# Threshold attention and a quick-GELU block on one core: masking moved to ScalarE, sums of weights folded on VectorE, values of a pair in one group

## Chip, core and metric

The kernel runs on one core of a Trainium2 chip. The metric is the device time of one execution in microseconds. Before the change it is 1937.87 us, the median of three runs (1936.68 to 1942.23).

## The reference

Attention over 8 batches and 8 heads with 576 positions of 64 elements, all fp32. A score counts only if it is within tau (0.02) of the largest of its row. Then a block with a quick GELU over the 4608 tokens, whose two weight matrices (512 x 2048 and 2048 x 512) come in as 64-bit floats.

```
scores = scale * q @ k.T
thresh = max(scores, -1) - tau
scores = where(scores >= thresh, scores, -1e9)
attn   = exp(scores - max(scores, -1))
x      = (attn / (sum(attn, -1) + 1e-9)) @ v      # heads side by side: 4608 x 512
h      = x @ w_in
out    = (h / (1 + exp(-1.702 * h))) @ w_out
```

## The kernel before

Two heads of a batch make a pair; there are 32 pairs. Scores are held transposed, with keys on partitions: four main tiles of 128 keys (128 x 1152, two heads side by side) and a tail tile, in which both heads have 64 partitions (128 x 576). Per pair:

- `prep` (L191) transposes q and k on VectorE in 32 x 32 blocks, and copies k's last 64 keys into a block-diagonal tile `kd`.
- `scores` (L207) has TensorE write two PSUM pairs and ScalarE copy them to SBUF. `part_max` (L233) takes maxima over 32 keys. `max_a`, `max_b` and `max_c` (L247 to L283) finish them over two TensorE transposes, and `mb` holds each query's maximum spread over 128 partitions.
- `sub` (L285) subtracts it, `exps` (L297) takes the exponential into another tile, `threshold` (L303) sets to zero what is under the threshold: one VectorE operation over two inputs.
- `values` (L311) multiplies by v on TensorE, tile by tile. `add_w` (L326) adds the tiles on GpSimd, `den_a` (L341) sums over partitions by a matmul with ones. `place_x` (L358) takes the reciprocal of 128 x 576 numbers and writes the scaled values as columns of x.

The second block runs over nine blocks of 512 tokens. A unit of `mm1` is two matmuls of 128x512 with w_in; every second one ends with a tanh on ScalarE (L389) and, on VectorE, gT (L390). A unit of `mm2` is two matmuls with w_out. Each fp32 matmul shows as two records in the trace. The PSUM tiles of both kinds (`hps`, `ops`) share two buffers.

The weights are made fp32 on the chip, in 64 pieces of 128 x 256. `convert_w` (L139) takes 24 bits of the mantissa on VectorE in two operations from both 32-bit words, the exponent in one more, which GpSimd limits and shifts; `convert_w_end` (L173) adds the sign, and GpSimd multiplies.

The order is written by hand, and each engine works through its own queue in that order. A step has a place in a period of 18 for its pair, and the steps are sorted by place (L445 to L497). The scores of one pair lie beside the values of the pair before. Pairs of the first batch have no units beside them; from then on each batch has the units of one block of the batch before. Two blocks are left for the end. All DMAs are issued by SP.

Of the kernel before, what the change touches and what calls it, by code (L numbers as in the profile page):

```python
# [11 lines left out]
U32 = mybir.dt.uint32  # L12
AF = mybir.ActivationFunctionType
# [7 lines left out]
BIG = 3.0e38  # L21


@with_exitstack
def kernel(
# [9 lines left out]
):  # L35

# [34 lines left out]
    psA = ctx.enter_context(tc.tile_pool(name="psA", bufs=2, space=bass.MemoryType.PSUM))  # L71
    psV = ctx.enter_context(tc.tile_pool(name="psV", bufs=1, space=bass.MemoryType.PSUM))
# [7 lines left out]
    ident = const.tile([P, P], FP32, name="ident")  # L80
    ones = const.tile([P, D], FP32, name="ones")
    tau_b = const.tile([P, 1], FP32, name="tau_b")
    neg = const.tile([P, 1], FP32, name="neg")
    scl = const.tile([P, 1], FP32, name="scl")
    ntau = const.tile([P, 1], FP32, name="ntau")
# [4 lines left out]
    def load_pair(n):  # L90
        b, hp = divmod(n, NPAIR)
        raws[n] = []
        for name, src in (("q", q), ("k", k)):
            t = work.tile([P, QB, 32], FP32, name=f"{name}_raw", tag=f"{name}_raw", bufs=1)
            for h in range(2):
                for j in range(2):
                    nc.sync.dma_start(
# [27 lines left out]
    def load_w():  # L125
# [6 lines left out]
        if not wide:  # L132
            nc.sync.dma_start(out=part, in_=dram)
            return
        t = work.tile([P, WC, 2], U32, name="w64", tag="w64", bufs=3)
        nc.sync.dma_start(out=t.rearrange("p c w -> p (c w)"), in_=dram.bitcast(U32))
        staged.append((t, part))

    def convert_w():  # L139

        if not staged:
            return
        t, part = staged.pop(0)
        lo, hi = t[:, :, 0], t[:, :, 1]

        frac = work.tile([P, WC], U32, name="frac", tag="frac")
        nc.vector.tensor_scalar(  # L147
            out=frac, in0=hi, scalar1=0xFFFFF, scalar2=4,
            op0=ALU.bitwise_and, op1=ALU.logical_shift_left,
        )  # L150
        nc.vector.scalar_tensor_tensor(  # L151
            out=frac, in0=lo, scalar=28, in1=frac,
            op0=ALU.logical_shift_right, op1=ALU.bitwise_or,
        )
        mant = work.tile([P, WC], FP32, name="mant", tag="mant")
        nc.scalar.activation(
            out=mant, in_=frac, func=AF.Copy, bias=1.0, scale=2.0**-24
# [31 lines left out]
    mats, sT, stats = {}, {}, {}  # L189

    def prep(n, which):  # L191
# [5 lines left out]
        if which == 1:  # L197
            for h in range(2):
                nc.gpsimd.tensor_copy(  # L199
                    out=kd[n % 2][ts(h, D), ts(h, D)], in_=dst[ts(h, D), MAIN:S]  # L200
                )
            del raws[n]
# [4 lines left out]
    def scores(n, t):  # L207
# [11 lines left out]
        else:  # L219
            st = work.tile([P, 2, S], FP32, name="s_m", tag="s_m", bufs=6)  # L220
# [12 lines left out]
    def part_max(n, t):  # L233

        if t == 0:
            stats[n] = [
                work.tile([P, NKT, 2 * QB], FP32, name="pmax", tag="pmax"),
# [73 lines left out]
    def values(n, t):  # L311
        if t == 0:
            pvs[n] = psV.tile([P, 2, 512], FP32, name="pv", tag="pv")
# [214 lines left out]
```

## Time and profile before

| | |
|---|---|
| median of three runs | 1937.87 us |
| profiled execution | 1936.7 us, of which the span 1934.9 us |
| TensorE, matmuls (PE) | 1596.7 us busy, 83% |
| VectorE (DVE) | 1271.3 us, 66% |
| ScalarE (ACT) | 500.4 us, 26% |
| GpSimd (POOL) | 553.2 us, 29% |
| chain that ended last | PE 50%, DVE 44% of the span |
| DMA | 12.3% of 16 engines' span, 55.47 MB |

The shares are means over stages with different limits, so the stages have to be read one by one. The profiled execution is 1.2 us under the median of the runs.

### The profile page before, as it was taken

Reading aid. Unit: us, or ns where it says so; the run is one execution under the profiler, and the core shown is the slowest. Engines: PE = TensorE matmul, PEld = TensorE weight load, DVE = VectorE, ACT = ScalarE, POOL = GpSimd, SP = SyncE. Lnnn points to the kernel's source line nnn. Section 1 sums busy time; section 2 is a strip of 40 time slices with the busy share of each in tenths; the row PEclk is TensorE's granted clock in tenths of the full one; section 3 lists DMA queues with packets and bytes.
Section 4 is the critical chain, followed back from the end, with each engine's and each line's share of the span. In section 5 each row is a group of like instructions: output and inputs, shape, how many; then the busy total and the mean of one; then the engine's idle time right before and its main releaser. Section 6 shows DMA issues by size and latency. Waiting matters only on the chain.

```text
span 1934.9 us, 14193 instructions
## 1 busy us (share of the span) xinstructions
PE 1596.7 (83%) x5056; PEld 688.1 (36%) x5056; DVE 1271.3 (66%) x1300; ACT 500.4 (26%) x725; POOL 553.2 (29%) x427
## 2 busy tenths in 40 slices
PE   4344477779888998899889998898889988999999
PEld 2122233334333333333333333333333333444444
DVE  7999989886766667766776666667666677521010
ACT  3222223222322223222322223223222332211010
POOL 3555555342222222222222221222222222200000
PEclk9766688889999998899999988999999988999999
DMA  3212222211111111111111110011111110000000
GB/s 81 54 47 57 62 57 62 57 38 30 24 19 23 31 24 19 19 30 30 19 19 28 31 19 5 20 30 24 19 19 29 30 19 6 12 11 6 16 0 22
DMA packets 205079, 55.47 MB, mean 29 GB/s; under 512 B 192208, under 2 KB 192208, under 8 KB 205008
## 3 DMA queue, kind: packets, MB, share of 16 engines
q1 hardware_dynamic: 205008, 54.56, 12.3%
q8 instruction: 40, 0.66, 0.1%
q14 instruction: 31, 0.25, 0.0%
HBM read 45.09 MB, written 9.44 MB: 28 GB/s over the span
## 4 chain that ended last, share of the span: by engine, by line
PE 50%; DVE 44%; issue 2%; ACT 2%; POOL 0%; SPq 0%; DVEq 0%; DMA 0%; ACTq 0%; POOLq 0%
PE ops L398 18%; PE hps L382 16%; DVE s_m L305 9%; DVE s_m L288 8%; PE pv L321 7%; PE ps L224 6%; DVE rc L361 6%; DVE s_t L291 5%; DVE frac L151 3%; DVE ex L177 2%; DVE qkT L195 2%; DVE mb L279 2%; DVE gT L390 2%; PE ps L213 2%; DVE frac L147 2%
## 5 line engine op out<-in xcount | busy, mean ns | idle before, releaser
L382 PE MATMUL hps<-xT,w_in 128*128 128x512 f32 x1152 | 583.8, 652 | 95.1 <-DVE gT L390 95.1
L398 PE MATMUL ops<-w_out,gT 128*128 128x512 f32 x1152 | 541.3, 617 | 27.9 <-DVE gT L390 27.9
L224 PE MATMUL ps<-qkT 64*128 64x288 f32 x1024 | 211.1, 496 | 196.6 <-ACT s_m L230 105.2
L382 PEld LDWEIGHTS hps<-xT,w_in 128*128 128x128 f32 x1152 | 224.6, 205 | 386.8 <-issue 257.6
L390 DVE SCALAR_TENSOR_TENSOR gT<-th,hps 128x512 f32<-128x512 f32 x144 | 98.6, 685 | 342.2 <-ACT th L389 342.2
L398 PEld LDWEIGHTS ops<-w_out,gT 128*128 128x128 f32 x1152 | 215.4, 195 | 295.4 <-issue 260.6
L199 POOL COPY kd<-qkT 64x64 f32<-64x64 f32 x64 | 62.8, 982 | 843.0 <-DVE qkT L195 743.8
L245 DVE TRANSPOSE_TENSOR_REDUCE pmax<-s_m 128x36 f32<-128x1152 f32 x128 | 172.8, 1364 | 117.6 <-ACT s_m L230 117.6
L300 ACT ACTIVATE e<-s_m,scl 128x1152 f32<-128x1152 f32 x128 | 160.7, 1256 | 331.4 <-DVE s_m L288 331.4
L305 DVE SCALAR_TENSOR_TENSOR s_m<-s_m,ntau,e 128x1152 f32<-128x1152 f32 x128 | 237.6, 1856 | 1.0
L224 PEld LDWEIGHTS ps<-qkT 64*128 64x128 f32 x1024 | 118.2, 213 | 306.2 <-issue 146.3
L230 ACT COPY s_m<-ps 128x576 f32<-128x576 f32 x256 | 151.8, 640 | 260.7 <-PE ps L224 260.7
L333 POOL TENSOR_TENSOR ws<-ws,s_m 128x1152 f32<-128x1152 f32 x64 | 183.6, 2868 | 64.6 <-DVE s_m L305 63.1
L288 DVE TENSOR_TENSOR s_m<-s_m,mb 128x1152 f32<-128x1152 f32 x128 | 172.4, 1348 | 2.5
L321 PE MATMUL pv<-s_m,v_m 128*64 128x288 f32 x1024 | 173.4, 465 | 0.0
L389 ACT ACTIVATE th<-hps 128x512 f32<-128x512 f32 x144 | 83.8, 590 | 203.8 <-PE hps L382 203.8
L361 DVE RECIPROCAL rc<-rc 128x576 f32<-128x576 f32 x32 | 119.8, 3745 | 12.5 <-ACT rc L352 12.5
L321 PEld LDWEIGHTS pv<-s_m,v_m 128*64 128x64 f32 x1024 | 69.2, 152 | 133.2 <-issue 109.2
L291 DVE TENSOR_TENSOR s_t<-s_t,mb 64x576 f32<-64x576 f32 x64 | 107.1, 1673 | 0.4
L331 POOL TENSOR_TENSOR ws<-s_m 128x1152 f32<-128x1152 f32 x32 | 90.6, 2830 | 37.9 <-DVE s_m L305 36.0
L337 POOL TENSOR_TENSOR ws<-ws,s_t 64x576 f32<-64x576 f32 x64 | 89.9, 1405 | 13.4 <-DVE s_t L305 9.4
L404 ACT ACTIVATE osb<-ops 128x512 f32<-128x512 f32 x36 | 21.2, 590 | 206.8 <-PE ops L398 206.8
(46 smaller groups left out, 837.3 us busy)
## 6 DMA issues: line engine op xcount, KB each, us to landing
q_raw<-in_q_dram SPq DMA_DIRECT2D x128, 72.0 KB, 2.4
k_raw<-in_k_dram SPq DMA_DIRECT2D x128, 72.0 KB, 2.4
out_dram<-osb SPq DMA_DIRECT2D x36, 256.0 KB, 2.0
v_m<-in_v_dram SPq DMA_DIRECT2D x64, 128.0 KB, 2.4
w<-in_moe_w_in_dram SPq DMA_DIRECT2D x32, 256.0 KB, 2.7
w<-in_moe_w_out_dram SPq DMA_DIRECT2D x32, 256.0 KB, 2.7
v_t<-in_v_dram SPq DMA_DIRECT2D x64, 16.0 KB, 2.1
tau_b<-in_tau_dram SPq DMA_DIRECT2D x1, 0.5 KB, 2.5
```

What stands on the lines that cost most here:

```text
L224: nc.tensor.matmul(ps[h][:, c, 0:SH], lhsT=kT[ts(h, D), ts(t, P)], rhs=qT[ts(h, D), ts(c, SH)], start=True, stop=True,)
L230: nc.scalar.copy(out=halves(st[:, h, :]), in_=ps[h][:, :, 0:SH])
L245: nc.vector.tensor_reduce(out=o, in_=i, axis=AXL.X, op=ALU.max, apply_transpose=True)
L288: nc.vector.tensor_tensor(out=s, in0=s, in1=mb, op=ALU.subtract)
L291: nc.vector.tensor_tensor(out=s[ts(h, D)], in0=s[ts(h, D)], in1=mb[ts(h, D), h, :], op=ALU.subtract)
L300: nc.scalar.activation(out=e, in_=s, func=AF.Exp, scale=scl)
L305: nc.vector.scalar_tensor_tensor(out=s, in0=s, scalar=ntau, in1=es.pop((n, t)), op0=ALU.is_ge, op1=ALU.mult)
L321: nc.tensor.matmul(pvs[n][ts(h, D), c, 0:SH], lhsT=lhsT, rhs=rhs, start=(t == 0), stop=(t == NKT),)
L333: nc.gpsimd.tensor_tensor(out=sums[n], in0=sums[n], in1=w[t], op=ALU.add)
L361: nc.vector.reciprocal(out=rc, in_=rc)
L382: nc.tensor.matmul(hidden[0], lhsT=w_in[:, c, ts(j, P)], rhs=xTs[blk][:, c, :], start=(c == 0), stop=(c == NDC - 1),)
L398: nc.tensor.matmul(acc[0], lhsT=gT[j][:, ts(i, P)], rhs=w_out[:, j, :], start=(j == 0), stop=(j == NFC - 1),)
```

## The change

- **Maxima and thresholds.** The two TensorE transposes go. `over_groups` folds the four groups of 32 partitions on VectorE by short copies and operations on 36 columns; `thresholds` subtracts the gap and spreads the result. `sub` then subtracts the threshold.
- **Masking.** ScalarE's parametric Relu with a slope of 1e30 keeps what is positive and drives what is negative far down; the Exp behind it, in place, has a bias that brings the gap back. The VectorE operation and the second tile `e` go.
- **Sums of weights.** GpSimd's additions go. For pairs 0 to 5 TensorE sums by a second group of 20 matmuls with ones; for the rest VectorE reduces each tile over 32 keys and folds as for the maxima. The reciprocal is taken of 18 columns, then spread.
- **Values.** All 20 matmuls of a pair follow each other, behind the first scores of the next pair. Their PSUM tile comes from the same pool as the scores', which now has three pairs of banks.
- **Weights.** A second load of each piece, shifted by three bytes, brings the mantissa's bits into one word, so one VectorE operation with one input replaces two. Nine conversions stand before the first units, the other 55 in 2.2 periods behind them; in the kernel before they stand in the first seven.
- **Other.** `kd` is copied by ScalarE, the first loads of k are issued by ScalarE's queue, score tiles have seven buffers instead of six. Places run on over all pairs instead of anew per pair.

```diff
-    psA = ctx.enter_context(tc.tile_pool(name="psA", bufs=2, space=bass.MemoryType.PSUM))
-    psV = ctx.enter_context(tc.tile_pool(name="psV", bufs=1, space=bass.MemoryType.PSUM))
+    psA = ctx.enter_context(tc.tile_pool(name="psA", bufs=3, space=bass.MemoryType.PSUM))
...
+        t3 = work.tile([P, WC, 2], U32, name="w64s", tag="w64s", bufs=3)
+        nc.sync.dma_start(
+            out=t3.rearrange("p c w -> p (c w)").bitcast(U8)[:, 0 : 8 * WC - 3],
+            in_=dram.bitcast(U8)[:, 3 : 8 * WC],
+        )
...
+        nc.vector.tensor_single_scalar(
+            out=frac, in_=t3[:, :, 0], scalar=0x0FFFFFFF, op=ALU.bitwise_and
+        )
...
+    def over_groups(n, op):
...
+        for w in (64, 32):
+            nc.vector.tensor_copy(out=o[0:w], in_=r[w : 2 * w])
+            nc.vector.tensor_tensor(out=r[0:w], in0=r[0:w], in1=o[0:w], op=op)
+        return r
...
-        e = work.tile(list(s.shape), FP32, name="e", tag="e")
-        nc.scalar.activation(out=e, in_=s, func=AF.Exp, scale=scl)
...
-        nc.vector.scalar_tensor_tensor(
-            out=s, in0=s, scalar=ntau, in1=es.pop((n, t)), op0=ALU.is_ge, op1=ALU.mult
-        )
...
+        nc.scalar.activation(out=s, in_=s, func=AF.Prelu, alpha=STEEP)
+        nc.scalar.activation(out=s, in_=s, func=AF.Exp, scale=scl, bias=shift)
...
+    def spread(n, r):
+
+        nc.vector.reciprocal(out=r, in_=r)
+        rc = work.tile([P, S], FP32, name="rc", tag="rc")
+        nc.vector.transpose(out=rc, in_=r.unsqueeze(2).to_broadcast([P, QB, 32]))
+        rcs[n] = rc
...
+    for n in range(NP):
+        t0 = LEN * n
+        for t in range(NKT + 1):
+            at(t0 + 1.5 * t, scores, n, t)
+            at(t0 + 1.5 * t + 1.0, in_groups, n, t, ALU.max)
+            at(t0 + 8.7 + 1.3 * t, sub, n, t)
+            at(t0 + 9.0 + 1.3 * t, exps, n, t)
+            if n >= BY_PE:
+                at(t0 + 12.4 + 1.3 * t, in_groups, n, t, ALU.add)
+        at(t0 + 8.0, thresholds, n)
+        at(t0 + 18.6, values, n)
+        at(t0 + 18.7, sums_by_pe if n < BY_PE else sums_by_dve, n)
+        at(t0 + 20.3, place_x, n)
...
+    for blk in range(NBLK):
+        first = ready(blk)
+        last = ready(blk + 1) if blk + 1 < NBLK else first + NPAIR * LEN
...
+            at(first + max(last - first, 1.0) * (u + 0.5) / len(todo), *unit)
...
+                at(begin + 0.7 * LEN * i / (early + 1), convert)
...
+                at(ready(0) + 2.2 * LEN * (i - early) / (len(pieces) - early), convert)
```

How the queues stand is shown at three places. First ScalarE, from the sums' eviction to the last exponential of a pair beside mm1 units; `th` is a unit's tanh, `rc` the sums. Before:

```order
L352 ACTIVATE rc<-den 128x576
L300 ACTIVATE e<-s_m,scl 128x1152
L389 ACTIVATE th<-hps 128x512
L300 ACTIVATE e<-s_m,scl 128x1152 x2
L389 ACTIVATE th<-hps 128x512
L300 ACTIVATE e<-s_m,scl 128x1152
L300 ACTIVATE e<-s_t,scl 128x576
```

With the change, in such a stretch from the second tile on (L300 is now the Prelu, L301 the Exp):

```order
L300 ACTIVATE s_m<-s_m 128x1152
L301 ACTIVATE s_m<-s_m,shift,scl 128x1152
L386 ACTIVATE th<-hps 128x512
L300 ACTIVATE s_m<-s_m 128x1152
L301 ACTIVATE s_m<-s_m,shift,scl 128x1152
L210 COPY kd_88<-qkT 64x64 x2
L300 ACTIVATE s_m<-s_m 128x1152
L301 ACTIVATE s_m<-s_m,shift,scl 128x1152
L386 ACTIVATE th<-hps 128x512
L300 ACTIVATE s_t<-s_t 128x576
L301 ACTIVATE s_t<-s_t,shift,scl 128x576
```

Each exponential has become two instructions, the tanh stands between two tiles as before, and the copies of `kd` are new in this queue.

Then TensorE behind the maxima of a pair beside mm1 units, where the next pair's scores and this pair's values begin. Before:

```order
L275 MATMUL p_3315<-ident,mq 128x36
L382 MATMUL hps<-xT,w_in 128x512 x16
L224 MATMUL ps<-qkT 128x288 x4
L382 MATMUL hps<-xT,w_in 128x512 x2
L321 MATMUL pv<-s_m,v_m 64x288 x4
L224 MATMUL ps<-qkT 128x288 x4
L382 MATMUL hps<-xT,w_in 128x512 x2
L321 MATMUL pv<-s_m,v_m 64x288 x4
```

With the change, from pair 6 on:

```order
L379 MATMUL hps<-xT,w_in 128x512 x22
L233 MATMUL ps<-qkT 128x288 x4
L315 MATMUL pv<-s_m,v_m 64x288 x16
L315 MATMUL pv<-s_t,v_t_89 64x288 x4
L379 MATMUL hps<-xT,w_in 128x512 x2
L233 MATMUL ps<-qkT 128x288 x4
```

Eleven units stand in one piece instead of eight, and the values have moved from between the tiles of scores into one group.

Last VectorE behind a pair's maxima while weights are converted; `mb` is the spread maximum or threshold, `frac` and `ex` belong to the conversion. Before:

```order
L279 STREAM_TRANSPOSE mb<-p_1184 128x1152
L177 SCALAR_TENSOR_TENSOR ex<-w_1064,ex 128x256
L147 TENSOR_SCALAR frac<-w_1101 128x256
L151 SCALAR_TENSOR_TENSOR frac<-w_1101,frac 128x256
L161 TENSOR_SCALAR ex<-w_1101 128x256
L288 TENSOR_TENSOR s_m<-s_m,mb 128x1152
L361 RECIPROCAL rc<-rc 128x576
```

With the change:

```order
L282 STREAM_TRANSPOSE mb<-thr 128x1152
L188 SCALAR_TENSOR_TENSOR ex<-w_990,ex 128x256
L162 TENSOR_SCALAR frac<-w64s 128x256
L172 TENSOR_SCALAR ex<-w_1005 128x256
L387 SCALAR_TENSOR_TENSOR gT_73<-th,hps 128x512
L291 TENSOR_TENSOR s_m<-s_m,mb 128x1152
L188 SCALAR_TENSOR_TENSOR ex<-w_1005,ex 128x256
L162 TENSOR_SCALAR frac<-w64s 128x256
L172 TENSOR_SCALAR ex<-w_1029 128x256
L188 SCALAR_TENSOR_TENSOR ex<-w_1029,ex 128x256
```

A conversion has one operation less, two of them now follow a subtraction, and the reciprocal of 576 columns is no longer in the queue.

## Rows read from the trace of the kernel before

**Rows 1.** Windows by stage: stretch, length, busy per engine (instructions), clock, DMA share, GB/s
```profile
24.00:224.60 200.60, 90.12 (x336) 44.14 (x336) 191.06 (x230) 57.84 (x89) 113.13 (x118) 0.69 0.23 57
224.60:417.50 192.90, 133.87 (x411) 57.07 (x411) 170.01 (x230) 55.28 (x93) 99.66 (x119) 0.82 0.21 55
417.50:1655.60 1238.10, 1084.13 (x3594) 458.96 (x3592) 848.18 (x769) 346.60 (x480) 323.83 (x169) 0.94 0.11 22
1655.60:1720.00 64.40, 64.40 (x192) 27.30 (x192) 30.62 (x28) 10.57 (x13) 12.45 (x5) 1.00 0.04 17
1720.00:1935.00 215.00, 211.13 (x492) 93.11 (x491) 20.61 (x30) 22.69 (x38) 0.00 (x0) 1.00 0.03 10
```
The busy times are, in order, those of PE, PEld (weight loads), DVE, ACT and POOL.

**Rows 2.** The same view: a window with mm1 units, one mostly with mm2
```profile
1134.80:1190.00 55.20, 46.52 (x151) 19.22 (x150) 38.82 (x38) 16.02 (x23) 12.50 (x7) 0.91 0.09 16
...
1242.60:1290.70 48.10, 43.99 (x151) 19.05 (x150) 31.77 (x29) 12.87 (x17) 14.46 (x7) 0.96 0.13 30
```

**Rows 3.** Waits: who for whom, us in total, times, longest
```profile
PE ps L224 <- ACT s_m L230: 105.2, 34, 7.4
...
PE hps L382 <- DVE gT L390: 95.1, 34, 5.3
```

**Rows 4.** Timeline of TensorE from 1126: start, length, instruction, [idle before <-releaser]
```profile
1126.85 1.98 PE L382 MATMUL hps<-xT,w_in 128*128 128x512 f32 x4
1128.77 1.19 PE L321 MATMUL pv<-s_m,v_m 128*64 128x288 f32 x8
...
1138.94 7.13 PE L382 MATMUL hps<-xT,w_in 128*128 128x512 f32 x16
1148.39 2.56 PE L382 MATMUL hps<-xT,w_in 128*128 128x512 f32 x4 [2.32 <-DVE gT L390]
```

**Rows 5.** VectorE's groups by form: busy us, mean ns of one | idle before
```profile
L305 DVE SCALAR_TENSOR_TENSOR s_m<-s_m,ntau,e 128x1152 f32<-128x1152 f32 x128 | 237.6, 1856 | 1.0
...
L245 DVE TRANSPOSE_TENSOR_REDUCE pmax<-s_m 128x36 f32<-128x1152 f32 x128 | 172.8, 1364 | 117.6 <-ACT s_m L230 117.6
L288 DVE TENSOR_TENSOR s_m<-s_m,mb 128x1152 f32<-128x1152 f32 x128 | 172.4, 1348 | 2.5
...
L361 DVE RECIPROCAL rc<-rc 128x576 f32<-128x576 f32 x32 | 119.8, 3745 | 12.5 <-ACT rc L352 12.5
...
L291 DVE TENSOR_TENSOR s_t<-s_t,mb 64x576 f32<-64x576 f32 x64 | 107.1, 1673 | 0.4
L390 DVE SCALAR_TENSOR_TENSOR gT<-th,hps 128x512 f32<-128x512 f32 x144 | 98.6, 685 | 342.2 <-ACT th L389 342.2
...
L279 DVE STREAM_TRANSPOSE mb<-p 128x1152 f32<-128x1152 f32 x32 | 44.3, 1383 | 35.4 <-PE p L275 35.4
...
L250 DVE TENSOR_REDUCE mx<-pmax 128x36 f32<-128x144 f32 x32 | 11.5, 358 | 0.0
L255 DVE TENSOR_TENSOR mx<-mx,pmax_t 64x18 f32<-64x18 f32 x64 | 11.0, 172 | 1.5
```

**Rows 6.** The same view: GpSimd's additions and ScalarE's Exp
```profile
L333 POOL TENSOR_TENSOR ws<-ws,s_m 128x1152 f32<-128x1152 f32 x64 | 183.6, 2868 | 64.6 <-DVE s_m L305 63.1
...
L300 ACT ACTIVATE e<-s_m,scl 128x1152 f32<-128x1152 f32 x128 | 160.7, 1256 | 331.4 <-DVE s_m L288 331.4
```

**Rows 7.** Line L291: ns min/median/max, first and last start us, form
```profile
L291 DVE TENSOR_TENSOR s_t<-s_t,mb x64: 740/791/3086, 41.7 to 1680.4; 64x576 f32<-64x576 f32 x64
```

**Rows 8.** Conversion: two groups by form, then line L177 as in rows 7
```profile
L151 DVE SCALAR_TENSOR_TENSOR frac<-w,frac 128x256 uint32<-128x256 uint32 x64 | 62.4, 974 | 2.2
...
L161 DVE TENSOR_SCALAR ex<-w 128x256 uint32<-128x256 uint32 x64 | 21.7, 338 | 0.0
...
L177 DVE SCALAR_TENSOR_TENSOR ex<-w,ex x64: 375/418/2835, 19.0 to 416.5; 128x256 uint32<-128x256 uint32 x64
```

**Rows 9.** DMA issues: KB each, median us from issue to landing
```profile
w<-in_moe_w_in_dram SPq DMA_DIRECT2D x32, 256.0 KB, 2.7
```

## What I expected before the run

> **What bounds the kernel now.** I first cut the span into stages by the starts of one instruction per pair, the maxima's reduce at L250. One period between two such starts I call a window; there are 32 pairs. Read in each row what is nearly full. From 24.0 to 224.6 us (four windows without matmuls of the second block, 50.2 us each) VectorE is busy 191.1 of 200.6 us: VectorE bounds. From 224.6 to 417.5 (three windows) it is still at 170.0 of 192.9, TensorE at 133.9. From 417.5 to 1655.6 (24 windows of 51.6 us) TensorE is busy 1084 of 1238 us at a granted clock of 0.94, VectorE 848. From 1720 on TensorE alone works, 211 of 215 us at clock 1.00 [rows 1]. In that last stretch nothing can be gained but by fewer matmuls, and the change takes none of those out.
>
> The 24 windows are the largest stage. Two of each four carry mm1 units (w_in, then tanh and gT), two carry mm2 units: the first row shown has mm1 (55.2 us), the second mostly mm2 (48.1 us). Read there that TensorE is busy 46.5 and 44.0 us, VectorE 38.8 and 31.8 [rows 2]. So TensorE is near its limit, and what can be won is its idle time and its half-speed stretches. Who makes it idle stands in the list of waits: ScalarE's evictions of the scores 105.2 us, VectorE's gT 95.1 us [rows 3]. The timeline shows one such wait: a stop of 2.32 us for gT, and the next four matmul records then last 2.56 us instead of 1.98, at the lower granted clock [rows 4].
>
> **The change on each engine.** All durations are of the profiled execution, 1936.7 us with a span of 1934.9; its time is 1.2 us under the median of the three runs, so the sum below stands for the median as well.
>
> VectorE loses, per pair, four masking operations of 1.856 us (7.4) and one of half the size, the 3.745 us reciprocal and, through it, the only long stop in its queue [rows 5]. It gains, from pair 6 on, four reductions of 1.36 us and one of half the size for the sums of the weights (6.2). The fold and the thresholds are some 20 operations on at most 36 columns per pair. They are not in the trace; the nearest rows are 0.172 us (64x18) and 0.358 us (128x144) [rows 5], so 3.4 to 7.2 us; I take 4, since the tiles are small like the first. Two visits to TensorE for transposes go. Net: VectorE saves about 5 us a window and 11 us while TensorE sums (pairs 0 to 5).
>
> GpSimd loses its additions, 2.87 us each [rows 6]. A half subtraction on VectorE has a median of 0.79 us but a maximum of 3.09 and a mean of 1.67 [rows 5, 7]: it stood behind such an addition. I take that back too, about 1.8 us a pair.
>
> ScalarE gains a Prelu beside each Exp. No row shows Prelu. Bounds: nothing less than an Exp-shaped pass without its pointer, and at worst two passes; I take 1.256 us, an ACTIVATE on the same tile on the same engine [rows 6], and keep 2.5 for the range. That makes some 2.55 us per tile, 11.6 per pair. The Trainium skill speaks against it: in "ScalarE: Activation LUTs", Rules for kernel authors, relu-like work belongs on VectorE. By that rule VectorE would mask cheaper than ScalarE; the rows differ, 1.856 us there against 1.256 here for fp32 with two inputs [rows 5, 6], so the sum keeps the rows.
>
> TensorE loses the four sums' matmuls (eight records, 1.19 us, as values' [rows 4]) and two transposes; while it sums itself (pairs 0 to 5) it gains five times eight records, 5.6 us, instead.
>
> **The sum, stage by stage.**
>
> *Start.* k's four loads go out on ScalarE's queue beside q's. Scores run with three PSUM pairs instead of two. I take the first thresholds at 19.5 us instead of 24.0 (ends: 17 and 24).
>
> *Four windows without mm1.* VectorE falls to some 21 us of work (31.8 less 11 [rows 2]), and nothing else is full, so the chain of one pair sets the window. Thresholds 3.5; first subtraction 1.35; five tiles through Prelu and Exp with the kd copies and hand-offs 13; last values 2; TensorE's sums 7.5 (5.6 at full clock, 11 at half; this stage's granted clock is 0.69 [rows 1]); reciprocal, MAX of the next pair and xT 5, which the next scores await, since the third PSUM pair holds pv; four more tiles of scores 8.6. That is 41 us. Window four holds nine conversions and the first mm1 units, +11. 3 x 41 + 52 = 175 instead of 200.6, to 194.5. Ends: 145 and 190.
>
> *Three windows with conversions.* 55 of 64 conversions now stand in 2.2 windows, 25 a window. VectorE's part of one: the third operation at its median 0.418 and two one-input ones of 0.338, no more 0.974 [rows 8]; 1.1 us, and up to 2 where the next must wait for GpSimd's operations (the third one's maximum is 2.8). I take 1.6: 25 x 1.6 = 40, and 27 of its own work (21 and eight gT), 67 to 68 us a window for two windows. The third has eight conversions and TensorE's last sums, 54. 68 + 68 + 54 = 190, much as now (192.9), to 384.5. Ends: 150 and 225.
>
> *24 windows.* TensorE's work: the mm2 row's 44.0 us less 1.2 and 0.5, and less the half-clock part (0.96), 41 us at full clock [rows 2, 4]. Does it run through? In an mm2 window the chain from thresholds to the last Exp is 3.5 + 1.35 + 12.5 = 17.4 us. TensorE has eleven units of 1.78 us (16 records in 7.13 [rows 4]), the next scores and four tiles of values to do meanwhile, 25 us: hidden. So 41. In an mm1 window a tanh stands in ScalarE's queue between two tiles, and gT behind it in VectorE's queue ahead of the next subtraction. Each such crossing costs gT 0.69 + subtraction 1.35 in which ScalarE idles [rows 5]; with the kd copies the chain grows to 26 or 27 us. gT is thereby late: TensorE has two hps buffers, and the unit two blocks on waits until some 22 us after the thresholds, having been ready at 16. That is 6 us of stop and nearly 2 at the lower clock: 41 + 8 = 49. Mean 45, and 24 x 45 = 1080 instead of 1238, to 1464.5. Ends: 41 (no stops) and 50 (Prelu two passes, or stops as today).
>
> *End.* The last chain 17.4, sums and xT 5, then the two blocks that stay: 512 matmul records at the pace of the 492 that now take 211.1 us [rows 1], 220; eviction and store 3.5. Together 246 (now 279.3, since more of the block before is done when the last thresholds come).
>
> Sum: 19.5 + 175 + 190 + 1080 + 246 = 1710.5, and 1.8 around the span: **1712 us**, 11.6% under now.
>
> What is late next: VectorE's queue waits for the shifted load at frac (L162), and behind it stand subtractions, gT and maxima, hence ScalarE and then values. 128 DMAs for weights where there were 64, of 256 KB each, on SP ahead of q, k and v; those are asked for a whole window before use. If that cover goes, prep waits 2.4 us or so per pair. The cover for ScalarE's 5.8 more microseconds per pair is the 25 us of TensorE work named above.
>
> **Rivals.**
>
> *A. TensorE runs through.* VectorE, rid of the reciprocal, brings gT in time and the mm1 windows take 41 as well: 12 x 8 = 96 less, 1616. For it: no long instruction is left in VectorE's queue. Against: the crossing of queues remains. Chance 0.15.
>
> *B. ScalarE's chain binds every window.* Prelu costs more than an Exp, or in-place operations cannot follow each other closely: 50 us a window, 24 x 5 = 120 more, 1832. For it: ScalarE gets two dependent passes per tile. Against: ScalarE is busy 16.0 of 55.2 us in the row [rows 2]. Chance 0.13.
>
> *C. Shifted loads are slow; slower than before.* A load of a weight piece lands 2.7 us after its issue [rows 9]. Rows that start 3 bytes off and hold 2045 bytes are not in the trace. Three staging buffers cover about two conversions, so a load of three times 2.7 puts 5.4 us on each of 55 conversions, 297 us: 2009. It decides from 1937 - 1712 = 225 us, 4.1 us per conversion, a load of 6.8 us. The Trainium skill, "DMA: Bandwidth & Descriptors", How a descriptor splits into AXI transactions, says that bytes below the start are fetched unused up to a 256 B boundary. By that rule a row from byte 3 to 2048 needs as many transactions as a whole one, and the time stays 1712; no run here shows it yet. Chance 0.06.
>
> *D. Little comes of it.* If VectorE's savings only turn into waits and a window stays near 51.6, the last stages give 1712 + 24 x 6.6 = 1870, still faster; to end level, the conversion windows would have to take 90 us too. Chance of level 0.02, of 1870 or so 0.04.
>
> **How the numbers follow.** My forecast has 0.60. The likeliest time is 1712. The low end takes in most of rival A and the short ends of the early stages, 1625; the high end takes in B, 1835. About 0.8 lies between; C and the rest are left out. A measurement of this kernel tells a change of 0.3% (6 us) from none. Faster: 0.60 + 0.15 + 0.13 + 0.04 = 0.92; level 0.02; slower 0.06.
>
> **What would show it.** Right: GpSimd idle after the conversions; the half subtraction near 0.75 us throughout; Prelu near 1.26; windows alternating near 49 and 41; in mm1 windows one TensorE stop of some 6 us for gT, and none for evictions in mm2 windows; VectorE near 65% in the long stage. Wrong: windows all alike, Prelu well over 1.3 us, frac waiting for DMAs by more than 2 us each, or a first stage that doesn't drop under 50 us a window. The forecast falls if the mean of the 24 windows is outside 41 to 50 us, or the three conversion windows take over 225.

## The result, and the profile after

The changed kernel takes 1717.97 us in the median of four runs (1716.00 to 1718.59), beside 1937.32 us for the kernel before (here the median of four runs): a ratio of 0.886, with a 95% interval of 0.8845 to 0.8877. The forecast was 1712 us in a range of 1625 to 1835. The profiled execution has a span of 1716.8 us.

First the page's busy times of the changed kernel, one line:

```profile
PE 1477.6 (86%) x4976; PEld 677.1 (39%) x4976; DVE 979.5 (57%) x1698; ACT 673.0 (39%) x917; POOL 117.1 (7%) x204
```

VectorE has lost 292 us and GpSimd 436; ScalarE has gained 173. TensorE has lost 119 us of busy time, with 4976 records now where there were 5056. Now the windows of the changed kernel by stage, cut at the same instruction (the reduce at L260 that begins a pair's fold of the maxima) and with the same columns as [rows 1]:

```profile
19.70:51.50 31.80, 19.05 (x116) 10.64 (x116) 19.74 (x32) 16.88 (x21) 0.00 (x0) 0.79 0.16 29
116.90:178.20 61.30, 36.25 (x148) 17.39 (x148) 35.28 (x79) 23.55 (x39) 28.08 (x45) 0.78 0.47 135
178.20:265.40 87.20, 55.45 (x179) 24.81 (x179) 47.87 (x118) 30.80 (x56) 46.80 (x79) 0.81 0.55 167
265.40:344.20 78.80, 53.98 (x181) 23.98 (x180) 43.82 (x104) 28.55 (x50) 40.54 (x70) 0.82 0.48 152
344.20:378.20 34.00, 33.66 (x128) 15.39 (x127) 27.20 (x46) 17.96 (x23) 0.34 (x1) 1.00 0.19 42
378.20:1463.50 1085.30, 984.96 (x3361) 449.46 (x3360) 714.98 (x1177) 478.00 (x624) 0.00 (x0) 0.95 0.12 25
1463.50:1716.80 253.30, 246.73 (x601) 108.67 (x600) 42.11 (x71) 36.11 (x52) 0.00 (x0) 1.00 0.03 11
```

| stage | before | forecast | after |
|---|---|---|---|
| to the first thresholds | 24.0 | 19.5 | 19.7 |
| four windows without mm1 | 200.6 | 175 | 158.5 |
| three windows with conversions | 192.9 | 190 | 200.0 |
| 24 windows | 1238.1 | 1080 | 1085.3 |
| end | 279.3 | 246 | 253.3 |

The first four windows are the first two rows and two more like the first, of 33.0 and 32.4 us. No engine is full in the two long conversion windows: read there TensorE 55.5, VectorE 47.9 and GpSimd 46.8 of 87.2 us. In the 24 windows TensorE is busy 985 of 1085 us. Four of those one by one, two with mm1 units and two with mm2, answer to [rows 2]:

```profile
781.10:832.70 51.60, 42.39 (x141) 19.05 (x140) 32.16 (x54) 21.76 (x29) 0.00 (x0) 0.93 0.10 18
832.70:881.90 49.20, 41.69 (x136) 18.67 (x135) 31.01 (x52) 20.56 (x27) 0.00 (x0) 0.90 0.10 18
881.90:920.80 38.90, 38.90 (x141) 18.13 (x140) 27.37 (x46) 18.08 (x23) 0.00 (x0) 1.00 0.17 37
920.80:962.00 41.20, 41.20 (x146) 19.07 (x145) 28.63 (x48) 19.27 (x25) 0.00 (x0) 1.00 0.16 35
```

With mm2 TensorE is busy to the last tenth at clock 1.00. With mm1 it stands still for 9.2 and 7.5 us, at clocks of 0.93 and 0.90. The list of waits says for whom (us in total, times, longest), beside [rows 3]:

```profile
ACT s_m L300 <- DVE s_m L291: 180.0, 48, 6.9
...
PE hps L379 <- DVE gT L387: 130.5, 30, 6.9
```

Over the whole span the 105.2 us in which TensorE waited for ScalarE's evictions have shrunk to 2.9, and the wait for gT has grown from 95.1 to 130.5. In the 24 windows alone it looks otherwise: the evictions held TensorE up for 46.6 us before and for none after, gT for 104.8 us before and 100.3 after. The 104.8 are 76.9 at `hps` and 27.9 at mm2's `ops`, a wait that [rows 3] don't have and that is gone after:

```profile
PE ops L398 <- DVE gT L390: 27.9, 6, 4.7
```

So in this stage the change took away the wait for evictions and left that for gT, which is now the only one. Now one such wait of the changed kernel in order of time (start, length, instruction, idle before and who ended it):

```profile
842.02 1.35 ACT L301 ACTIVATE s_m<-s_m,shift,scl 128x1152 f32<-128x1152 f32 x1
843.27 0.58 ACT L386 ACTIVATE th<-hps 128x512 f32<-128x512 f32 x1
843.88 0.69 DVE L387 SCALAR_TENSOR_TENSOR gT<-th,hps 128x512 f32<-128x512 f32 x1 [4.26 <-ACT th L386]
844.49 1.35 DVE L291 TENSOR_TENSOR s_m<-s_m,mb 128x1152 f32<-128x1152 f32 x1
844.63 5.40 PE L379 MATMUL hps<-xT,w_in 128*128 128x512 f32 x8 [3.48 <-DVE gT L387]
...
845.88 1.17 ACT L300 ACTIVATE s_m<-s_m 128x1152 f32<-128x1152 f32 x1 [2.02 <-DVE s_m L291]
```

The tanh `th` stands in ScalarE's queue behind the Exp. VectorE waits 4.26 us for it; meanwhile the next subtraction, which needs nothing from `th`, stands behind gT. When gT has run, TensorE goes on, but its eight records take 5.40 us and not 3.70; and ScalarE has stood idle for 2.02 us, waiting for that subtraction. Last, the masking pair and the two kinds of subtraction among the groups of instructions:

```profile
L301 ACT ACTIVATE s_m<-s_m,shift,scl 128x1152 f32<-128x1152 f32 x128 | 172.4, 1347 | 4.3
...
L300 ACT ACTIVATE s_m<-s_m 128x1152 f32<-128x1152 f32 x128 | 148.1, 1157 | 180.4 <-DVE s_m L291 180.0
...
L294 DVE TENSOR_TENSOR s_t<-s_t,mb 64x576 f32<-64x576 f32 x64 | 48.8, 763 | 0.4
```

Prelu takes 1.157 us and the Exp behind it 1.347, together 2.504 where the forecast had some 2.55. The half subtraction has fallen from a mean of 1.673 [rows 5] to 0.763 us.

### The profile page after: what moved, and what is told of

It is laid out like the page before. It is cut to its first block, busy times and chain, and to the rows that moved or that the text cites. A ratio compares the mean times of both kernels' runs of the same rounds, so it can differ in the third digit from the quotient of the medians.

```text
span 1716.8 us, 14214 instructions
## 1 busy us (share of the span) xinstructions
PE 1477.6 (86%) x4976; PEld 677.1 (39%) x4976; DVE 979.5 (57%) x1698; ACT 673.0 (39%) x917; POOL 117.1 (7%) x204
## 4 chain that ended last, share of the span: by engine, by line
PE 66%; DVE 16%; ACT 9%; POOL 4%; issue 3%; DMA 1%; SPq 1%; DVEq 0%; POOLq 0%; ACTq 0%
PE ops L395 28%; PE hps L379 19%; PE pv L315 8%; PE ps L233 7%; DVE s_m L291 4%; ACT s_m L301 3%; ACT s_m L300 3%; DVE part L254 2%; PE den L315 2%; DVE gT L387 2%; ACT th L386 1%; PE ps L222 1%; DVE mb L282 1%; DVE qkT L206 1%; POOL ex L176 1%
## 5 line engine op out<-in xcount | busy, mean ns | idle before, releaser
L379 PE MATMUL hps<-xT,w_in 128*128 128x512 f32 x1152 | 580.1, 656 | 140.9 <-DVE gT L387 130.5
L395 PE MATMUL ops<-w_out,gT 128*128 128x512 f32 x1152 | 514.0, 597 | 2.1 <-ACT osb L401 2.1
L254 DVE TRANSPOSE_TENSOR_REDUCE part<-s_m 128x36 f32<-128x1152 f32 x232 | 316.0, 1363 | 140.8 <-ACT s_m L239 132.3
L233 PE MATMUL ps<-qkT 64*128 64x288 f32 x1024 | 171.8, 442 | 65.7 <-DVE qkT L206 61.8
L300 ACT ACTIVATE s_m<-s_m 128x1152 f32<-128x1152 f32 x128 | 148.1, 1157 | 180.4 <-DVE s_m L291 180.0
L301 ACT ACTIVATE s_m<-s_m,shift,scl 128x1152 f32<-128x1152 f32 x128 | 172.4, 1347 | 4.3
L291 DVE TENSOR_TENSOR s_m<-s_m,mb 128x1152 f32<-128x1152 f32 x128 | 170.9, 1364 | 0.6
L315 PE MATMUL pv<-s_m,v_m 128*64 128x288 f32 x1024 | 136.1, 420 | 0.1
L315 PE MATMUL den<-s_m,ones 128*64 128x288 f32 x192 | 32.8, 510 | 25.6 <-ACT s_m L239 25.6
L254 DVE TRANSPOSE_TENSOR_REDUCE part_t<-s_t 128x18 f32<-128x576 f32 x58 | 44.8, 772 | 14.0 <-ACT s_t L226 12.6
L188 DVE SCALAR_TENSOR_TENSOR ex<-w,ex 128x256 uint32<-128x256 uint32 x64 | 26.7, 418 | 43.7 <-POOL ex L179 43.4
L294 DVE TENSOR_TENSOR s_t<-s_t,mb 64x576 f32<-64x576 f32 x64 | 48.8, 763 | 0.4
L282 DVE STREAM_TRANSPOSE mb<-thr 128x1152 f32<-128x1152 f32 x32 | 44.1, 1378 | 1.1
```

Source lines behind the costliest of these rows:

```text
L233: nc.tensor.matmul(ps[h][:, c, 0:SH], lhsT=kT[ts(h, D), ts(t, P)], rhs=qT[ts(h, D), ts(c, SH)], start=True, stop=True,)
L254: nc.vector.tensor_reduce(out=o, in_=i, axis=AXL.X, op=op, apply_transpose=True)
L282: nc.vector.transpose(out=mb.rearrange("p h s -> p (h s)"), in_=f.unsqueeze(2).to_broadcast([P, 2 * QB, 32]),)
L291: nc.vector.tensor_tensor(out=s, in0=s, in1=mb, op=ALU.subtract)
L300: nc.scalar.activation(out=s, in_=s, func=AF.Prelu, alpha=STEEP)
L301: nc.scalar.activation(out=s, in_=s, func=AF.Exp, scale=scl, bias=shift)
```

## The experiments

Each kernel is the changed one with the edit shown; ratios are to the kernel before, measured beside it. The changed kernel's own is 0.886. "The 24 windows" are counted between the starts of the spread threshold `mb` (L282 in the changed kernel), where the changed kernel has 1085.3 us. The windows with mm2 took 41.2 and 38.9 us in every kernel below but the one with all sums on TensorE, so their times can be compared with each other.

### Subtractions ahead of gT

```diff
-            at(t0 + 8.7 + 1.3 * t, sub, n, t)
+            at(t0 + 8.7 + 0.3 * t, sub, n, t)
```

> The changed kernel with the five subtractions of a pair placed 0.3 apart instead of 1.3, so that they stand ahead of the gT of the same stretch. Theory 1 (the queues of ScalarE and VectorE cross at tanh and gT, and each crossing leaves ScalarE without a subtracted tile): ScalarE's stops of 2 us before a Prelu in mm1 windows go, TensorE's stops for gT shrink, mm1 windows fall from 49 to 51 us to 45 or 46, mm2 windows stay at 39 to 41; 1655 to 1670 us. Theory 2 (ScalarE's own load, two passes a tile and the tanh, makes gT late): the order of the subtractions changes nothing, 1710 to 1726 us.

Measured: 1660.78 us, ratio 0.858 (0.8559 to 0.8601). The 24 windows fell by 65 us; two with mm1:

```profile
768.00:814.20 46.20, 39.52 (x142) 18.03 (x141) 32.08 (x55) 21.54 (x29) 0.00 (x0) 1.00 0.11 20
814.20:858.00 43.80, 38.79 (x136) 17.52 (x135) 30.71 (x52) 20.34 (x27) 0.00 (x0) 0.96 0.12 21
```

No work was taken away; only the order on VectorE changed. Of the 10.8 us that these two windows lost, TensorE's stops account for 5.0 (16.7 to 11.7 us by the list of waits) and TensorE's shorter busy time at the higher clock for 5.8. That the subtraction behind gT holds these windows up is shown. Over the 24 windows 40 us of stops went and, with the same number of records, 25 us of busy time: a stop cost about 1.6 times its length. Two windows alone don't tell that ratio, since windows of the same 46.1 us here held between 3.8 and 6.7 us of stops. The first seven windows became 8 us longer.

### Masking back on VectorE

```diff
-        nc.scalar.activation(out=s, in_=s, func=AF.Prelu, alpha=STEEP)
-        nc.scalar.activation(out=s, in_=s, func=AF.Exp, scale=scl, bias=shift)
+        e = work.tile(list(s.shape), FP32, name="e", tag="e")
+        nc.scalar.activation(out=e, in_=s, func=AF.Exp, scale=scl, bias=shift)
...
+        nc.vector.scalar_tensor_tensor(
+            out=s, in0=s, scalar=0.0, in1=es.pop((n, t)), op0=ALU.is_ge, op1=ALU.mult
+        )
...
+            at(t0 + 10.4 + 1.3 * t, threshold, n, t)
```

Score tiles have six buffers, and the spread reciprocal shares `e`'s.

> The changed kernel with the masking alone undone: Exp into a second tile, then one VectorE operation with two inputs; six score tiles instead of seven, the reciprocal's tile shares the second tile's buffers. VectorE gets 7 to 9 us a pair back, ScalarE loses 5.8. Theory 1 (TensorE's work bounds the mm2 windows, the crossing of queues the mm1 windows): mm2 windows stay near 41, mm1 windows grow by 0 to 4; 1718 to 1780 us. Rival (VectorE's busy time sets the window, so its saved 9 us were the gain): 24 to 28 windows by 7 us more, 1870 to 1930 us.

Measured: 1693.21 us, ratio 0.875 (0.8723 to 0.8777): 25 us less than the changed kernel, and outside what either theory said. The masking product took 1.374 us, not the 1.856 of before [rows 5]: its scalar is now a constant and no longer a pointer, and GpSimd's additions beside it are gone; which of these it was isn't shown. The 24 windows fell by 42 us, all of it with mm1. The stops of one window, where the changed kernel had 3.48 and 5.73 us (781.1 to 832.7):

```profile
793.47 3.70 PE L388 MATMUL hps<-xT,w_in 128*128 128x512 f32 x8 [1.12 <-DVE gT L396]
802.99 5.53 PE L388 MATMUL hps<-xT,w_in 128*128 128x512 f32 x8 [5.82 <-DVE gT L396]
```

The first stop is shorter, since the tanh stands behind Exps alone; the second stays. So ScalarE's Prelu isn't free: it delays the tanh. The first seven windows pay 17 us of it back. No run has six buffers alone, so what the missing buffer costs here and in the next two kernels isn't shown.

### Both of these

The two diffs above, together.

> The two edits that each shortened the windows with the first layer, together: the subtractions of a pair stand ahead of gT's product in VectorE's order, and the masking is a VectorE product after the Exp. Theory 1 (both shorten the same crossing of ScalarE's and VectorE's orders around th and gT, by different parts: the one ScalarE's wait for the subtraction, the other the 5.8 us of Prelu that th stands behind): the windows with the first layer fall from 46.2 and 43.8 (subtractions early) to 42 to 44 and 40 to 42, 30 to 50 less than with the subtractions early alone: 1612 to 1640. Rival (they remove the same wait, and VectorE's five more products cost what is left): within 10 of the subtractions early alone, 1651 to 1671.

Measured: 1690.51 us, ratio 0.875 (0.8722 to 0.8786). Both theories fall: it is 30 us slower than the early subtractions alone. Of these, 17 us lie in the first seven windows, where masking on VectorE cost 17 in the other order too, and 13 in the 24 windows. For the 13 the trace of this kernel names a new crossing:

```profile
797.70 0.58 ACT L395 ACTIVATE th<-hps 128x512 f32<-128x512 f32 x1
798.86 1.51 DVE L294 TENSOR_TENSOR s_t<-s_t,mb 64x576 f32<-64x576 f32 x2
800.41 1.36 DVE L308 SCALAR_TENSOR_TENSOR s_m<-s_m,e 128x1152 f32<-128x1152 f32 x1
801.68 0.68 DVE L396 SCALAR_TENSOR_TENSOR gT<-th,hps 128x512 f32<-128x512 f32 x1
...
802.42 6.70 PE L388 MATMUL hps<-xT,w_in 128*128 128x512 f32 x8 [4.49 <-DVE gT L396]
```

The tanh is done at 798.28 us, but gT starts at 801.68, behind the half subtractions and a masking product. With the subtractions out of the way, ScalarE is the better place for the mask in the 24 windows; with them in the way, VectorE was.

### GpSimd's additions as idle work

```diff
+    def add_w(n, t):
...
+            nc.gpsimd.tensor_tensor(out=sums[n], in0=sums[n], in1=w[t], op=ALU.add)
...
+                at(t0 + 12.4 + 1.3 * t, add_w, n, t)
```

From pair 6 on GpSimd adds the tiles again, into a tile that nothing reads; score tiles have six buffers.

> The changed kernel with GpSimd's five additions put back beside everything else from pair 6 on; nothing reads their result, so only what they take from others shows. Six score tiles instead of seven. Theory 1 (an addition keeps VectorE's two-input operations waiting, and in mm1 windows they stand in the chain): the half subtraction's mean goes from 0.76 to over 1.3 us, mm1 windows grow by 1.5 to 4, mm2 windows by 0 to 1; 1735 to 1775 us. Rival (the waits lie in VectorE's slack): the mean rises but the time stays, 1712 to 1726 us.

Measured: 1731.29 us, ratio 0.894 (0.892 to 0.8964), 13 us more than the changed kernel and between the two expectations. The subtractions in this kernel:

```profile
L291 DVE TENSOR_TENSOR s_m<-s_m,mb 128x1152 f32<-128x1152 f32 x128 | 189.8, 1512 | 1.5
L294 DVE TENSOR_TENSOR s_t<-s_t,mb 64x576 f32<-64x576 f32 x64 | 94.2, 1472 | 0.9
```

The half subtraction went from 0.763 to 1.472 us. So additions on GpSimd do slow VectorE, as the forecast read from [rows 7]; but the 24 windows took only 9.5 us more, 0.4 each.

### The reciprocal of 576 columns

```diff
-        nc.vector.reciprocal(out=r, in_=r)
...
+        nc.vector.reciprocal(out=rc, in_=rc)
```

> The changed kernel with the reciprocal alone taken over 576 columns again, 3.7 us instead of 0.27. Theory 1 (it stands after the last Exp, where VectorE has slack; only pv's PSUM pair and one gT wait for it): 0 to 1 us a window from pair 4 on, about 1 us in each of the first four, 1718 to 1745 us. Rival (it stopped VectorE's queue on the path in every window): 32 times 3.5 us, 1815 to 1835 us.

Measured: 1738.03 us, ratio 0.898 (0.8956 to 0.9002), within theory 1's range. Where it went is seen in the two stages, this kernel's 24 windows and its first seven:

```profile
401.30:1484.60 1083.30, 984.52 (x3361) 449.26 (x3360) 796.75 (x1176) 477.99 (x624) 0.00 (x0) 0.95 0.12 25
...
22.40:401.30 378.90, 245.82 (x986) 116.87 (x987) 238.63 (x439) 151.73 (x229) 115.53 (x192) 0.81 0.38 107
```

VectorE got 82 us more work in the 24 windows, which took no longer (1083.3 beside 1085.3). All of the 20 us lie in the first seven (378.9 beside 358.6). 13 of them are in the four without mm1, 3.2 us each: there the chain of one pair sets the time, and the rival's 3.5 us was nearer than theory 1's one.

### No shifted load

```diff
-            out=frac, in_=t3[:, :, 0], scalar=0x0FFFFFFF, op=ALU.bitwise_and
+            out=frac, in0=hi, scalar1=0xFFFFF, scalar2=4,
+            op0=ALU.bitwise_and, op1=ALU.logical_shift_left,
...
+            out=frac, in0=lo, scalar=28, in1=frac,
+            op0=ALU.logical_shift_right, op1=ALU.bitwise_or,
```

The second loads go.

> The byte-shifted loads are gone; a weight's fraction is put together again by two VectorE operations on the lower and the upper words (64 more of the one kind and one of another, 0.2 to 0.45 us each, some 20 to 27 us of VectorE's work in all). Theory 1 (the shifted loads hide behind the conversion's round trips over GpSimd and cost little; removing a VectorE operation is worth at most what VectorE is late by): the time rises by 5 to 25 us over the change's 1718, to 1723 to 1743, all of it in the three conversion windows. Rival (the second 4 MB of loads, or their landing time, paces the conversion): the time falls by 10 or more, to 1708 or less, and the conversion windows shrink from 87, 79 and 34 us.

Measured: 1740.73 us, ratio 0.901 (0.8971 to 0.9055), so theory 1. VectorE got more work than expected, since the second operation took 0.887 us each. The two conversion windows took 98.1 and 86.9 us instead of 87.2 and 78.8, although half of the loads were gone:

```profile
186.50:284.60 98.10, 61.04 (x180) 26.54 (x180) 69.61 (x144) 31.04 (x55) 44.01 (x78) 0.76 0.27 79
```

In the changed kernel the page gives the time from issue to landing as the last number, for plain and shifted loads:

```profile
w<-in_moe_w_in_dram SPq DMA_DIRECT2D x32, 256.0 KB, 3.2
w<-in_moe_w_out_dram SPq DMA_DIRECT2D x32, 256.0 KB, 2.9
w64s<-in_moe_w_in_dram SPq DMA_DIRECT2D x32, 255.6 KB, 3.5
w64s<-in_moe_w_out_dram SPq DMA_DIRECT2D x32, 255.6 KB, 3.3
```

A shifted load, issued right behind the plain one, landed 0.3 to 0.4 us later; without shifted loads the plain ones landed in 2.7 and 2.8 us. The rule that the prediction took from the Trainium skill ("DMA: Bandwidth & Descriptors", How a descriptor splits into AXI transactions) agrees with these rows, as far as times tell; no run here counts transactions.

### Conversions sooner

```diff
-        early, begin = 8, ready(0) - 0.7 * LEN
+        early, begin = 32, ready(0) - 2.7 * LEN
```

with the spread over 2.7 periods instead of 0.7.

> 32 of the 64 conversions are placed in the first three windows, where TensorE runs at 0.79 of its clock and VectorE, GpSimd and the queues are idle for half of the time, in place of 8 placed just before the first block. Theory 1 (the conversion windows of 87 and 79 us are paced by the conversions' round trips): the two windows fall to some 60 to 68 us each, the first windows rise from 32 to 36 to 42 us; in sum 20 to 40 less, 1678 to 1698. Rival (they are paced by the matmuls of the first block at a lower clock and by the waits for gT, not by the conversions): within 8 of the change, 1710 to 1726.

Measured: 1701.80 us, ratio 0.881 (0.8774 to 0.8847), 16 less than the changed kernel and between the expectations. The two long windows fell to 64.2 and 55.6 us and the fourth from 61.3 to 53.0, but the second and third rose to 43.9 and 54.1, further than theory 1 had it. So the conversions did pace the two windows; they pace the early ones as well, if less.

### All sums on TensorE

```diff
-    BY_PE = 6
+    BY_PE = 32
```

> The weights' sums of all 32 pairs are made by TensorE's matmuls with ones instead of those of the first six only; VectorE loses five to six transposing reductions of 1.36 us in each of 26 pairs. Theory 1 (TensorE's work sets the windows): some 5.0 us of TensorE more in 26 pairs, so 100 to 135 more, 1818 to 1853; the windows with the second layer rise from 38.9 and 41.2 to 44 to 46. Rival (VectorE's work sets the windows with the first layer): these shrink by 3 to 6 us, those with the second layer rise by 5, and the sum is 0 to 50 more, 1718 to 1768.

Measured: 1800.00 us, ratio 0.932 (0.9278 to 0.936), 82 more, between the two. A window with mm1 and one with mm2:

```profile
817.70:869.90 52.20, 45.82 (x181) 21.43 (x180) 25.25 (x39) 21.76 (x29) 0.00 (x0) 0.97 0.10 18
963.70:1009.70 46.00, 46.00 (x187) 22.06 (x186) 21.36 (x34) 19.87 (x26) 0.00 (x0) 1.00 0.14 32
```

The 5 us are paid in full with mm2 (41.2 to 46.0), where TensorE runs through. With mm1 the windows are 1.3 us longer in the mean of twelve (50.4 to 51.7), since TensorE had stops to put the work into.

### Early subtractions and sooner conversions

The diffs of the first kernel and of the conversions, together.

> The subtractions early and the 32 earlier conversions, together; they act in different windows. Theory 1 (the gains add: 57 us and 16 us): 1641 to 1651. Rival (each took the same waits in the conversion windows): 1655 to 1665, no better than the subtractions early alone.

Measured: 1645.53 us, ratio 0.850 (0.8475 to 0.853), so theory 1: the gains add.

### A tanh between every two tiles

```diff
-            at(t0 + 9.0 + 1.3 * t, exps, n, t)
+            at(t0 + 8.9 + 2.25 * t, exps, n, t)
...
-                at(t0 + 12.4 + 1.3 * t, in_groups, n, t, ALU.add)
+                at(t0 + 10.0 + 2.1 * t, in_groups, n, t, ALU.add)
```

on top of the kernel above.

> As the run above it, but ScalarE's masking and Exp of a pair's tiles are placed 2.25 instead of 1.3 places apart (and the sums' reductions likewise), so that one Tanh stands between two tiles instead of behind two. Theory 1 (what is left of the stops in a window with the first layer, 3.5 and 3.2 us, is a Tanh behind two tiles of Prelu and Exp, 5.0 us): both stops go, the windows with the first layer fall from 46.1 and 43.8 to 40 to 43, so 36 to 72 us less than the run above it: 1575 to 1610. Rival (the Tanhs wait for something else, or the values that now come later take it back): within 10 of the run above it, 1636 to 1656.

Measured: 1646.59 us, ratio 0.850 (0.8481 to 0.8523), so the rival's time. The 24 windows took 1013.6 us instead of 1020.4, and the seven before gave 10 back. The tanh did come sooner:

```profile
761.97 5.15 DVE L291 TENSOR_TENSOR s_m<-s_m,mb 128x1152 f32<-128x1152 f32 x4
...
765.80 0.58 ACT L386 ACTIVATE th<-hps 128x512 f32<-128x512 f32 x1
...
768.58 1.38 DVE L254 TRANSPOSE_TENSOR_REDUCE part<-s_m 128x36 f32<-128x1152 f32 x1
769.88 0.65 DVE L387 SCALAR_TENSOR_TENSOR gT<-th,hps 128x512 f32<-128x512 f32 x1
...
770.58 8.83 PE L379 MATMUL hps<-xT,w_in 128*128 128x512 f32 x16 [4.48 <-DVE gT L387]
```

The tanh is done at 766.38, gT starts at 769.88, behind the subtractions and a reduction. The queue that is late has changed from ScalarE's to VectorE's.

### Both queues in turn, then the products first

```diff
-            at(t0 + 8.7 + 0.3 * t, sub, n, t)
+            at(t0 + 8.7 + (0.3 if n < BY_PE else 0.8) * t, sub, n, t)
...
-            at(t0 + 9.0 + 1.3 * t, exps, n, t)
+            at(t0 + (9.0 + 1.3 * t if n < BY_PE else 8.9 + 2.25 * t), exps, n, t)
...
-                at(t0 + 12.4 + 1.3 * t, in_groups, n, t, ALU.add)
+                at(t0 + 12.0 + 1.65 * t, in_groups, n, t, ALU.add)
```

on top of early subtractions and sooner conversions, so that three subtractions precede gT from pair 6 on. The copies to `kd` are GpSimd's from pair 7 on.

> As the run before with masks spread, from the seventh pair on alone, and now on both engines: VectorE's subtractions stand 0.8 places apart, so that gT's product comes behind three of them instead of behind all six and a reduction, the sums' reductions begin later, and the copies to kd are GpSimd's. Theory 1 (a Tanh that comes in time is worth nothing as long as its product with the hidden values stands behind VectorE's subtractions; with both in turn the stops go): the windows with the first layer fall from 46.1 and 43.8 us to 40 to 43 each, so 25 to 65 less than the 1645.5 of early subtractions and sooner conversions: 1580 to 1620. Rival (something else sets these windows, the two output buffers of the first layer or the values' wait for the last mask): within 10 of it, 1635 to 1656.

Measured: 1620.75 us, ratio 0.839 (0.8351 to 0.8435): 25 less, just short of theory 1's range. The 24 windows took 993.9 us, and stops of 1.05 and 2.30 us stayed in a window with mm1. Then, on top:

```diff
-                at(t0 + 12.0 + 1.65 * t, in_groups, n, t, ALU.add)
+                at(t0 + 13.2 + 1.35 * t, in_groups, n, t, ALU.add)
...
-            at(t0 + 12.0, prep, n + 1, 0)
-            at(t0 + 12.6, prep, n + 1, 1)
+            at(t0 + (12.0 if n < BY_PE else 13.3), prep, n + 1, 0)
+            at(t0 + (12.6 if n < BY_PE else 13.9), prep, n + 1, 1)
```

with the two loads behind them, at 14.0 and 14.1.

> As the run before, with the next pair's transposes, its loads and the sums' reductions placed after the second product of a window, not ahead of it: what still stood ahead of gT's product there was half a tile's subtraction, one reduction and two transposes, 4.4 us, and TensorE stopped 2.3 us for it and 1.05 us for the first product. Theory 1 (the rest of the stops is the same crossing): 1 to 2.3 us less in each of 12 windows, 1592 to 1610. Rival (the later transposes make the next pair's scores late, or TensorE's own work now sets these windows): within 5 of it, 1616 to 1626.

Measured: 1562.33 us (1561.62 to 1562.54), ratio 0.806 (0.8043 to 0.8074), 58 less: the way that theory 1 said, and well below its range. Its windows with mm1, one with mm2, and the 24 together:

```profile
718.40:758.60 40.20, 39.15 (x141) 17.96 (x140) 31.83 (x54) 20.71 (x27) 0.47 (x2) 1.00 0.13 23
758.60:796.50 37.90, 36.86 (x136) 16.84 (x135) 30.58 (x51) 18.92 (x24) 0.47 (x2) 1.00 0.13 24
796.50:835.50 39.00, 39.00 (x142) 18.21 (x141) 27.40 (x47) 17.59 (x21) 0.47 (x2) 1.00 0.17 37
...
360.60:1310.30 949.70, 937.13 (x3362) 433.24 (x3361) 710.46 (x1177) 459.66 (x576) 11.23 (x48) 1.00 0.14 29
```

TensorE is busy 937 of 950 us at clock 1.00, with as many matmul records as the changed kernel (3362 beside 3361). Of the 55 us between the two profiled spans, 44 lie in these windows (993.9 to 949.7) and 11 in the seven before, where the next pair's loads were moved too; what those 11 are made of wasn't tried apart, nor which of the moved steps bought the 44. This version beats both kernels.

## Why the forecast came out

- **Start:** 19.5 forecast, 19.7 measured.
- **Four windows without mm1:** the step that fails is the sum of 41 us for one pair's chain; it took 32 to 33. The second of these windows shows where (`den` are the sums):

```profile
70.84 4.05 PE L315 MATMUL den<-s_m,ones 128*64 128x288 f32 x32
...
74.72 1.14 PE L315 MATMUL den<-s_t,ones_t 128*64 128x288 f32 x8
...
75.78 0.75 PE L233 MATMUL ps<-qkT 64*128 64x288 f32 x2
...
79.19 0.85 DVE L366 TENSOR_TENSOR xT<-pv,rc 128x288 f32<-128x288 f32 x3
```

  The sums took 5.0 us where I had 7.5 (and five times the 1.19 us of [rows 4] are 5.95, not 5.6). The next scores start at 75.78, right behind them, and don't await the reciprocal, the MAX and xT, which ends at 80.04. From the end of the sums to the next thresholds, 8.7 us went by instead of 5 and 8.6. So the wait for xT was not there, and that is 4.9 of the 8 us. The fourth window was 61.3 instead of 52: nine conversions and the first units cost some 29 us on top of 32.4, where I had added 11.
- **Conversion windows:** the reasons were half right. VectorE isn't full as I had it (47.9 of 87.2 us, where I had 67 to 68 us of work fill the window); a conversion goes back and forth between VectorE, GpSimd and ScalarE, and VectorE's last operation of each waited 43.4 us in all for GpSimd. That the conversions pace these windows is shown by placing some of them sooner; which of their waits does it isn't. 200 us instead of 190: 166 in the two long windows where I had 136, and 34 in the third where I had 54. Saving an operation (the shifted load) was worth 23 us, and moving conversions into earlier windows 16.
- **24 windows:** 45.2 us in the mean for 45. My list of waits [rows 3] was of the whole span; of its 105.2 and 95.1 us, 46.6 and 76.9 lay in these windows. VectorE's saving came as forecast (35.3 to 29.8 us a window, for about 5). The mm2 windows were 38.9 and 41.2 for 41, and TensorE ran through, as argued. The mm1 windows were 50.4 in the mean for 49, but by other terms. At clock 1.00 their 141 and 136 records take 39.2 and 36.9 us (the last kernel), 38.0 in the mean where I had 41; the stops were 8.4 us a window where I had 6, and the lower clock cost 4.0 where I had nearly 2. That these errors nearly cancel is luck. The mechanism, the queues of ScalarE and VectorE crossing at `th` and gT, is shown by the early subtractions (65 us less) and by the last kernel, where the stops were all but gone. The form was off: two stops in each of these windows, of 3.48 and 4.03 us in the one shown, instead of one of 6.
- **"The cover for ScalarE's 5.8 more microseconds":** right for mm2, where masking costs nothing (41.2 and 38.9 us with the mask on either engine). In mm1 windows Prelu adds to what the tanh stands behind; masking on VectorE in this order was 25 us faster, 42 of it gained there and 17 lost in the first seven windows. The Trainium skill's rule ("ScalarE: Activation LUTs", Rules for kernel authors) that relu-like work belongs on VectorE thus gave the better time here, though not by the price of an operation alone: 1.157 us on ScalarE, 1.374 on VectorE. With early subtractions the same move made the 24 windows 13 us slower, so there the order decides and not the rule.
- **End:** 253.3 for 246. The two blocks that stay began 26 us after the last thresholds, where I had 22.4 for the chain, sums and xT; the rest took 227 instead of 223.5.
- **Rivals:** A (TensorE runs through) was no property of this change, but of an order that it didn't have; the last kernel reaches it, and by more than the 96 us that A gave; A's own 1616 lay below my low end of 1625, so the range didn't take it in as I wrote. B fell by Prelu's 1.157 us and by the Exp that follows it at once (4.3 us of idle time before 128 of them). C fell by the shifted loads' 3.3 to 3.5 us where it needed 6.8; `frac` waited for them three times, 13.6 us in all. D didn't come.
- **Not tried:** no run takes back the third pair of PSUM banks, the values in one group or the fold in place of TensorE's transposes. What each of them gives of the 219 us, and which of them ended the wait for evictions, stays open. Of the parts that were taken back one by one, the short reciprocal is worth 20 us, the shifted load 23, and masking on ScalarE costs 25 in this order.

The errors were -16.5, +10, +5 and +7 us by stage behind the start. That the total missed by 6 is partly luck: the first stage's error cancels most of the others.

## What to carry to other kernels

When a wait for a product recurs, look at what stands ahead of it in its engine's queue but doesn't feed it; here the order, with the small copies to `kd` moved to GpSimd, was worth 136 us of the 24 windows' 1085, without one operation fewer. Moving work to an idle engine is priced by what stands behind it there, not by its own length alone: in these windows the same Prelu was the better choice in one order and the worse in another. Where TensorE is full, work put on it counts in full (5 us a window). Where it stops for others, the stop cost about 1.6 times its length here, since matmuls behind it ran at a lower clock: from the changed kernel to the last one the 24 windows lost 88 us of stops and 48 of busy time, at clocks of 0.95 and 1.00.

## What I had not expected of the hardware

After its long stops TensorE's next eight records of 512 columns took longer than the 3.70 us that eight take at clock 1.00: 5.40 after 3.48 us, 6.47 after 4.03, 6.70 after 5.73 and after 4.49, 5.53 after 5.82. After 1.12 us they took 3.70; one stop of 3.48 us elsewhere in the changed kernel was followed by 3.70, so the length of the stop alone doesn't tell it. Three of these, from two windows of the changed kernel:

```profile
792.97 3.70 PE L379 MATMUL hps<-xT,w_in 128*128 128x512 f32 x8 [3.48 <-DVE gT L387]
802.40 6.70 PE L379 MATMUL hps<-xT,w_in 128*128 128x512 f32 x8 [5.73 <-DVE gT L387]
...
854.05 6.47 PE L379 MATMUL hps<-xT,w_in 128*128 128x512 f32 x8 [4.03 <-DVE gT L387]
```
